# Ten query products of the late half-steps summed whole by VectorE, and the last value product summed in one strided instruction

## The chip, the cores and the metric

The kernel runs on one core of one Trainium2 chip. The core has five engines, each with its own queue of instructions: TensorE (matrix products; PE in the profile, and PEld for its weight loads), VectorE (DVE), ScalarE (ACT), GpSimd (POOL) and SyncE (SP, which here issues most of the DMA transfers). They run side by side and wait for each other through semaphores. The metric is the device time of one execution in microseconds (us); lower is better.

## The reference

Four layers, each added to its input, work on one sequence of 2048 positions with 640 features in float32. Layers 1 and 3 are a local attention, layers 2 and 4 a Fourier mixing; both attention layers use the same weights.

```python
x = A_x
x = x + _A_ref(_layernorm(x, axis=-1), A_wqkv, A_wo)
x = x + _B_ref(_layernorm(x, axis=-1), ...)
x = x + _A_ref(_layernorm(x, axis=-1), A_wqkv, A_wo)
x = x + _B_ref(_layernorm(x, axis=-1), ...)

def _A_ref(x, wqkv, wo):            # H = 32 heads of Dh = 20, W = 8, dil = 2
    ...
    idx = pos[:, None] - off[None, :]            # the 8 positions pos - 0, 2, .. 14
    kg = k[:, :, idx_c, :].reshape(B, H, S, W, Dh)
    vg = v[:, :, idx_c, :].reshape(B, H, S, W, Dh)
    logits = jnp.einsum("bhsd,bhswd->bhsw", q, kg) * scale
    logits = jnp.where(mask[None, None, :, :], logits, -1e9)
    attn = _softmax(logits, axis=-1)
    o = jnp.einsum("bhsw,bhswd->bhsd", attn, vg)
    return (lambda x, *d: x.transpose(*d))(o, 0, 2, 1, 3).reshape(B, S, D) @ wo

def _B_ref(x, dft_seq_re, dft_seq_im, dft_hid_re, dft_hid_im):
    a = jnp.einsum("bsd,ed->bse", x, dft_hid_re)
    b = jnp.einsum("bsd,ed->bse", x, dft_hid_im)
    return jnp.einsum("ts,bse->bte", dft_seq_re, a) - jnp.einsum("ts,bse->bte", dft_seq_im, b)
```

## The kernel before

**Tiling.** The even positions are put ahead of the odd ones, so that a step of two becomes a step of one. A chunk `c` (four of them) is 512 positions: 128 partitions of four neighbouring positions `j`. Every large matrix product is made of three TensorE passes over a high and a low part of each operand; ScalarE makes the high part, and VectorE, GpSimd or TensorE the low one.

**The attention layer** (`layer_a`, lines 242 to 863) is cut into 32 units `u`, each one group of four heads (80 features) of one chunk, and a unit into two half-steps, s = 2u + jp, of two of the four positions. So a layer has 64 half-steps, and what is called a step in the code is one half-step. In the last eight units (`PAIRED`) a unit holds two head groups for the same two positions; the work of a half-step is the same. For each half-step there are:

- a query product (`qk_mul`, L431): VectorE multiplies the queries, which ScalarE has copied into PSUM (`q_copy`, L404), with the window of eight keys, 1280 elements on each partition: 2 positions, 8 window places, 4 heads, 20 features;
- a halving (L433): GpSimd adds the features 10 to 19 of every head to the features 0 to 9, in place;
- a reduction (`qk_red`, L439), one step later: VectorE sums the ten that are left to one logit, 64 logits on each partition;
- the softmax on VectorE and ScalarE (`soft`, L454 to L464, `soft_exp`, L447), once for a unit;
- three steps later a weight product (`av_mul`, L469): VectorE multiplies the attention weights with the window of eight values, 1280 elements again;
- a tree (`av_tree`, L484 to L486): GpSimd adds the eight window places in three sums of 640, 320 and 160 elements; the last one writes 80 features into the output tile `zo`. For the very last product of a layer VectorE makes the three sums itself.

The products lie in four buffers `pr0` to `pr3`, taken in turn; a half-step takes two of them (one for L431, one for L469), so that a buffer comes back after two half-steps. The windows `win` have five buffers, which DMA fills ahead (L417).

**Beside these steps** TensorE makes the query, key and value projections of later chunks (L362), the transposes of inputs and outputs (L327, with L335 for the low part), the output projection (L509, added to the residual by VectorE at L159), and in the late steps it begins the next layer's transform along the sequence (L956). For that one, matrices are loaded (`c_load`, L912) and split by ScalarE (L916) and GpSimd or VectorE (`c_lo`, L943); layer normalised inputs are split by ScalarE (L885) and GpSimd or VectorE (`ln_lo`, L889).

**Order.** In an attention layer the order on all engines is the program's own: a table `plan` gives each piece of work a step and a phase, and `PHASES` orders the phases of a step. Each engine works its list strictly in that order. In a step of odd number the reduction (`red1`) comes after the query product, in one of even number (`red0`) ahead of it. After step 66 the last two output tiles are written out by hand: transposes of `zo` (`pc_pe(67)`), the rest of the output projection and the normalisation.

**Names that the change touches:** `qk_mul`, `qk_red`, `av_tree`, and a new table `WHOLE` beside `LEAD2`. `ly` is 0 in the first attention layer and 1 in the second; `NG` is 32, so `(NG - 1, 1)` is the last half-step.

Of the kernel before, what the change touches and what calls it, by code (L numbers as in the profile page):

```python
# [14 lines left out]
ALU = mybir.AluOpType  # L15
AX = mybir.AxisListType
# [18 lines left out]
FE = 80  # L35
# [8 lines left out]


LEAD2 = (-7, -6, -5, -4, -2, -1, 0, 0, 1, 1, 2, 3, 3, 4, 5, 5)
ZTHIRDS = (
    {49: 3, 50: 3, 51: 2, 53: 3, 54: 1, 56: 3, 57: 6, 58: 3, 59: 4, 60: 2, 61: 1, 62: 3, 63: 4, 64: 1, 55: 0, 52: 0},
    {50: 3, 51: 5, 52: 1, 53: 1, 54: 1, 55: 1, 56: 5, 57: 4, 58: 3, 59: 3, 60: 1, 61: 1, 62: 4, 63: 2, 64: 4},
# [25 lines left out]
def tile_layers(ctx: ExitStack, tc: tile.TileContext, x, wqkv, wo, cs, wre, wim, out):  # L75
    nc = tc.nc
# [13 lines left out]
    def T(shape, tag, dt=F32, bufs=1, pool=None):  # L90
        return (pool or sb).tile(shape, dt, tag=tag, name=nm(tag), bufs=bufs)
# [146 lines left out]
    NG = NC * NE  # L238
# [3 lines left out]
    def layer_a(li, stats, handoff, prev):  # L242
        xin, xout = xs[li], xs[li + 1]
        first = li == 0
        ly = li // 2
# [10 lines left out]
        prq = {}  # L256
        avq = {}
        oo = {}
# [8 lines left out]
        def prod():  # L267
            pcnt[0] += 1
            return T([P, 2, W, FE], f"pr{pcnt[0] % 4}")
# [114 lines left out]
        def half(u, i):  # L384
            if u in PAIRED:
                q, jp = PAIRED[u]
                return 2 * q + i, jp
            return u % NE, i
# [35 lines left out]
        def wview(u, i, t, tail):  # L424
            w, off = win.pop((u, i, t))
            return bass.AP(tensor=w.tensor, offset=w.offset + off, ap=[w.ap[0], [FE, 2], [FE, W]] + tail)

        def qk_mul(u, jp):
            pr = prod()
            q = qs[u][:, 2 * jp : 2 * jp + 2].unsqueeze(2).to_broadcast([P, 2, W, FE])  # L430
            nc.vector.tensor_tensor(pr, q, wview(u, jp, 0, [[1, FE]]), op=ALU.mult)  # L431
            pv = pr.rearrange("p j w (h d) -> p (j w h) d", d=DH)
            nc.gpsimd.tensor_tensor(pv[:, :, 0:10], pv[:, :, 0:10], pv[:, :, 10:20], op=ALU.add)  # L433
            prq[(u, jp)] = pv

        def qk_red(u, jp):
            if jp == 0:
                lgs[u] = T([P, NJ, W, HE], "lg", bufs=2)
            nc.vector.tensor_reduce(  # L439
                lgs[u][:, 2 * jp : 2 * jp + 2].rearrange("p j w h -> p (j w h)"),  # L440
                prq.pop((u, jp))[:, :, 0:10],
                axis=AX.X,
                op=ALU.add,
            )
# [32 lines left out]
        def av_tree(u, i):  # L477
            c = u // NE
            e, jp = half(u, i)
            if e == 0:  # L480
                oo[(c, jp)] = T([P, 2, D], f"zo{(2 * c + jp) % 4}")
            pr = avq.pop((u, i))
            g = nc.vector if (u, i) == (NG - 1, 1) else nc.gpsimd
            g.tensor_tensor(pr[:, :, 0:4], pr[:, :, 0:4], pr[:, :, 4:8], op=ALU.add)  # L484
            g.tensor_tensor(pr[:, :, 0:2], pr[:, :, 0:2], pr[:, :, 2:4], op=ALU.add)  # L485
            g.tensor_tensor(oo[(c, jp)][:, :, e * FE : (e + 1) * FE], pr[:, :, 0], pr[:, :, 1], op=ALU.add)  # L486

        def r_load(c, j, tag="xr"):
            xr[(c, j)] = load_x(xin[c], j, tag)
# [182 lines left out]
        o = NJ * FE + NJ * W * HE  # L672
# [21 lines left out]
        ]  # L694
        gs = list(LEAD0 if first else LEAD2)
        tx = {(0, j): -8 for j in range(NJ)}
        st = 4
        while len(gs) < NGRP:
            if st % 2 == 0 and len(tx) < NC * NJ:
                c, j = divmod(len(tx), NJ)  # L700
# [16 lines left out]
        for u in range(NG):  # L717
            if u in PAIRED:
                for i in range(2):
                    at(2 * u + i - 2, "dmaw", w_load, u, 0, i)  # L720
                    at(2 * u + i + 1, "dmaw", w_load, u, 1, i)
            else:
                at(2 * u - 2, "dmaw", w_load, u, 0)
                at(2 * u + 1, "dmaw", w_load, u, 1)
            at(2 * u - 1, "qc", q_copy, u)
            at(2 * u - 2, "dma", q_load, u)
            for jp in range(2):
                s = 2 * u + jp
                at(s, "qk", qk_mul, u, jp)
                at(s + 1, "red0" if jp else "red1", qk_red, u, jp)  # L730
                at(s + 3, "av0" if jp else "av1", av_mul, u, jp)
                at(s + 3, "av0" if jp else "av1", av_tree, u, jp)
            for i, ph in enumerate(("sA", "sB", "sC")):
                at(2 * u + 2, ph, soft, u, i)
                at(2 * u + 3, ("sD", "sE", "sF")[i], soft, u, 3 + i)
            at(2 * u + 2, "exp", soft_exp, u)
# [65 lines left out]
        last = 66  # L802
        thirds = [t for t, n in ZTHIRDS[ly].items() for _ in range(n)]
        for z, (tag, t) in PRE.items() if first else ():
# [552 lines left out]
```

## Time and profile before

| | us |
|---|---|
| runs before | 1794.40, 1787.53, 1791.88; median 1791.88 |
| the profiled execution, as a run | 1791.85 |
| its span in the profile | 1790.0 |
| mean granted TensorE clock | 0.995 of full speed |

| engine | busy us | share of the span | instructions |
|---|---|---|---|
| TensorE, matmuls (PE) | 1740.7 | 97% | 8798 |
| TensorE, weight loads (PEld) | 1506.0 | 84% | 8798 |
| VectorE (DVE) | 1380.2 | 77% | 2137 |
| ScalarE (ACT) | 813.0 | 45% | 1690 |
| GpSimd (POOL) | 636.4 | 36% | 595 |

A name such as `DVE lg L439` in the profile is an engine, the tile that it writes and the line of the kernel. `lg<-pr 128x64 f32<-128x640 f32 x128 | 103.9, 812 | 18.2` is a group of instructions: output and input by name, their shapes (partitions x elements), how many, busy time in us, the mean of one in ns, and the engine's idle time just before them. Busy times over the span are averages over stages that differ, so the stretches of the attention layers are read by themselves: the first one runs from about 30 to 390 us, the second from about 930 to 1280 us. An instruction's end in the profile can overlap the next one's start by a little, since the engines pipeline.

### The profile page before, as it was taken

Reading aid. Unit: us, or ns where it says so; the run is one execution under the profiler, and the core shown is the slowest. Engines: PE = TensorE matmul, PEld = TensorE weight load, DVE = VectorE, ACT = ScalarE, POOL = GpSimd, SP = SyncE. Lnnn points to the kernel's source line nnn. Section 1 sums busy time; section 2 is a strip of 40 time slices with the busy share of each in tenths; the row PEclk is TensorE's granted clock in tenths of the full one; section 3 lists DMA queues with packets and bytes.
Section 4 is the critical chain, followed back from the end, with each engine's and each line's share of the span. In section 5 each row is a group of like instructions: output and inputs, shape, how many; then the busy total and the mean of one; then the engine's idle time right before and its main releaser. Section 6 shows DMA issues by size and latency. Waiting matters only on the chain.

```text
span 1790.0 us, 26461 instructions
## 1 busy us (share of the span) xinstructions
PE 1740.7 (97%) x8798; PEld 1506.0 (84%) x8798; DVE 1380.2 (77%) x2137; ACT 813.0 (45%) x1690; POOL 636.4 (36%) x595
## 2 busy tenths in 40 slices
PE   9999998989999999999999999999999999999999
PEld 7889887778888888888888889888788888888888
DVE  6999998887767767767728999989777677677683
ACT  4664544454445445445523344444534443443441
POOL 4899999940000000000007998889300000000000
PEclk9999999999999999999999999999999999999999
DMA  7896678757778777787737866687687777876761
GB/s 246 286 313 203 211 212 270 251 183 281 273 251 258 246 265 253 238 272 255 216 107 220 285 205 209 211 303 254 218 298 263 254 226 225 265 230 224 257 208 52
DMA packets 271849, 425.15 MB, mean 238 GB/s; under 512 B 22592, under 2 KB 150592, under 8 KB 271456
## 3 DMA queue, kind: packets, MB, share of 16 engines
q1 hardware_dynamic: 268512, 421.49, 71.9%
q10 hardware_dynamic: 3200, 1.97, 0.4%
q8 instruction: 70, 1.15, 0.3%
q14 instruction: 67, 0.55, 0.1%
HBM read 338.23 MB, written 85.14 MB: 237 GB/s over the span
## 4 chain that ended last, share of the span: by engine, by line
PE 59%; DVE 15%; POOL 10%; DMA 9%; issue 3%; ACT 2%; SPq 0%; ACTq 0%; DVEq 0%; POOLq 0%
PE aux L1034 13%; PE m L362 11%; PE m L1123 10%; PE t L1123 10%; PE pq L1123 5%; PE xt L1123 5%; DVE pr L431 4%; POOL pr L484 3%; DVE pr L469 3%; POOL pr L433 2%; DMA win<-cs_in 2%; POOL pr L485 2%; PE aux L509 2%; DMA xc<-stg 1%; DVE lg L439 1%
## 5 line engine op out<-in xcount | busy, mean ns | idle before, releaser
L362 PE MATMUL m<-r,s 128*128 128x480 f32 x1920 | 438.0, 383 | 4.2 <-ACT s L232 3.7
L362 PEld LDWEIGHTS m<-r,s 128*128 128x128 f32 x1920 | 356.4, 189 | 58.3 <-ACT s L232 4.6
L174 POOL TENSOR_TENSOR stats<-stats,mhalf 128x1 f32<-128x1 f32 (+1 forms) x40 | 29.8, 745 | 564.1 <-ACT stats L170 554.8
L1116 ACT CAST r<-win 128x512 fp32r<-128x512 f32 x248 | 151.2, 619 | 169.2 <-DVE win L1152 78.3
L1034 PE MATMUL aux<-r2a,zo 128*128 128x320 f32 x768 | 226.4, 310 | 0.0
L484 POOL TENSOR_TENSOR pr<-pr 128x640 f32<-128x640 f32 x126 | 205.1, 1628 | 30.6 <-DVE pr L469 29.8
L1034 PE MATMUL aux<-pr,zo 128*128 128x320 f32 x704 | 208.2, 308 | 0.0
L1117 DVE TENSOR_TENSOR r<-win,r 128x512 fp32r<-128x512 f32 x248 | 167.6, 688 | 44.9 <-ACT r L1116 42.9
L431 DVE TENSOR_TENSOR pr<-pq,win 128x1280 f32<-128x1280 f32 x128 | 189.8, 1483 | 15.9 <-ACT pq L404 12.7
L469 DVE TENSOR_TENSOR pr<-pq,win 128x1280 f32<-128x1280 f32 x128 | 190.9, 1491 | 4.3
L433 POOL TENSOR_TENSOR pr<-pr 128x640 f32<-128x640 f32 x128 | 183.8, 1436 | 14.1 <-DVE pr L431 13.7
L1123 PE MATMUL m<-r,r 128*128 128x512 f32 x606 | 156.2, 392 | 0.7 <-DVE r L1117 0.7
L1034 PEld LDWEIGHTS aux<-r2a,zo 128*128 128x128 f32 x768 | 144.1, 188 | 2.0
L1123 PEld LDWEIGHTS m<-r,r 128*128 128x128 f32 x606 | 113.6, 188 | 26.2 <-DVE r L1117 1.0
L1034 PEld LDWEIGHTS aux<-pr,zo 128*128 128x128 f32 x704 | 132.1, 188 | 2.1
L1123 PE MATMUL t<-r,r 128*128 128x512 f32 x483 | 130.7, 393 | 2.3 <-issue 1.3
L956 PE MATMUL m<-s,r 128*128 128x512 f32 x384 | 119.0, 397 | 11.3 <-DMA s<-c0b 3.9
L956 PE MATMUL t<-s,r 128*128 128x512 f32 x384 | 119.2, 398 | 2.3 <-DVE ot L1016 1.5
L439 DVE TENSOR_REDUCE lg<-pr 128x64 f32<-128x640 f32 x128 | 103.9, 812 | 18.2 <-POOL pr L433 18.0
L485 POOL TENSOR_TENSOR pr<-pr 128x320 f32<-128x320 f32 x126 | 112.9, 896 | 9.9
L1123 PEld LDWEIGHTS t<-r,r 128*128 128x128 f32 x483 | 90.5, 188 | 23.7 <-issue 1.7
L369 ACT COPY stg<-m 128x480 f32<-128x480 f32 x128 | 70.9, 554 | 81.6 <-PE m L362 58.9
(285 smaller groups left out, 3227.7 us busy)
## 6 DMA issues: line engine op xcount, KB each, us to landing
win<-cs_in SPq DMA_DIRECT2D x354, 256.0 KB, 4.2
r<-xc SPq DMA_DIRECT2D x240, 256.0 KB, 4.3
win<-kvb SPq DMA_DIRECT2D x96, 440.0 KB, 4.5
xa<-cs_in SPq DMA_DIRECT2D x122, 256.0 KB, 4.3
win<-kvb SPq DMA_DIRECT2D x64, 360.0 KB, 5.1
xc<-stg SPq DMA_DIRECT2D x40, 512.0 KB, 3.8
kvb<-stg SPq DMA_DIRECT2D x60, 320.0 KB, 4.6
xr<-xs SPq DMA_DIRECT2D x41, 320.0 KB, 3.7
```

Source lines behind the costliest of these rows:

```text
L362: nc.tensor.matmul(mt[g][:, : 3 * F], st[:, a, k], wq[q][:, b, k], start=n == 0, stop=n == 14)
L431: nc.vector.tensor_tensor(pr, q, wview(u, jp, 0, [[1, FE]]), op=ALU.mult)
L433: nc.gpsimd.tensor_tensor(pv[:, :, 0:10], pv[:, :, 0:10], pv[:, :, 10:20], op=ALU.add)
L439: nc.vector.tensor_reduce(lgs[u][:, 2 * jp : 2 * jp + 2].rearrange("p j w h -> p (j w h)"), prq.pop((u, jp))[:, :, 0:10], axis=AX.X, op=AL ...
L469: nc.vector.tensor_tensor(pr.rearrange("p j w (h d) -> p j w h d", d=DH), lgs[u][:, 2 * jp : 2 * jp + 2].unsqueeze(4).to_broadcast([P, 2, ...
L484: g.tensor_tensor(pr[:, :, 0:4], pr[:, :, 0:4], pr[:, :, 4:8], op=ALU.add)
L485: g.tensor_tensor(pr[:, :, 0:2], pr[:, :, 0:2], pr[:, :, 2:4], op=ALU.add)
L956: self.last = nc.tensor.matmul(self.z[t][k], self.xn[c][:, a, j, k * P : (k + 1) * P], self.ct[s][:, b], start=s == 0 and i == 0, stop=s = ...
L1034: self.last = nc.tensor.matmul(self.ym[e][:, :320], zt[(k, a, ri)][:, j2 * P : (j2 + 1) * P], w[:, e * 320 : (e + 1) * 320], start=(k, a, ...
L1116: nc.scalar.copy(hi, raw)
L1117: nc.vector.tensor_tensor(lo, raw, hi.bitcast(F32), op=ALU.subtract)
L1123: nc.tensor.matmul(bank, w(a, kb), hl[b], start=start and (a, b) == (0, 0), stop=stop and (a, b) == (1, 0),)
```

## The change

For ten half-steps, listed in `WHOLE` (eight in the first attention layer: 43, 45, 47, 49, 51, 55, 57 and 59; two in the second: 51 and 57), GpSimd's halving is left out, and VectorE's reduction reads all twenty features of a head in place of ten. For the last weight product of each attention layer, VectorE's three sums become one reduction over the window axis, whose eight terms lie 80 elements apart. Everything else, and the order of the remaining instructions on every engine, is as it was. The kernel after has 10 GpSimd instructions fewer and 4 VectorE instructions fewer.

```diff
+WHOLE = ((43, 45, 47, 49, 51, 55, 57, 59), (51, 57))
...
             pv = pr.rearrange("p j w (h d) -> p (j w h) d", d=DH)
-            nc.gpsimd.tensor_tensor(pv[:, :, 0:10], pv[:, :, 0:10], pv[:, :, 10:20], op=ALU.add)
+            if 2 * u + jp not in WHOLE[ly]:
+                nc.gpsimd.tensor_tensor(pv[:, :, 0:10], pv[:, :, 0:10], pv[:, :, 10:20], op=ALU.add)
+                pv = pv[:, :, 0:10]
             prq[(u, jp)] = pv
...
                 lgs[u][:, 2 * jp : 2 * jp + 2].rearrange("p j w h -> p (j w h)"),
-                prq.pop((u, jp))[:, :, 0:10],
+                prq.pop((u, jp)),
                 axis=AX.X,
                 op=ALU.add,
...
             pr = avq.pop((u, i))
-            g = nc.vector if (u, i) == (NG - 1, 1) else nc.gpsimd
+            o = oo[(c, jp)][:, :, e * FE : (e + 1) * FE]
+            if (u, i) == (NG - 1, 1):
+                nc.vector.tensor_reduce(o, pr.rearrange("p j w f -> p j f w"), axis=AX.X, op=ALU.add)
+                return
+            g = nc.gpsimd
             g.tensor_tensor(pr[:, :, 0:4], pr[:, :, 0:4], pr[:, :, 4:8], op=ALU.add)
             g.tensor_tensor(pr[:, :, 0:2], pr[:, :, 0:2], pr[:, :, 2:4], op=ALU.add)
-            g.tensor_tensor(oo[(c, jp)][:, :, e * FE : (e + 1) * FE], pr[:, :, 0], pr[:, :, 1], op=ALU.add)
+            g.tensor_tensor(o, pr[:, :, 0], pr[:, :, 1], op=ALU.add)
```

## The prediction

> **What bounds the kernel now.** I read the page first, then busy time by stretch, then the chain of waits and who waited for whom in the late half-steps, and last the single instructions. The 40 slices of the page are 44.75 us each.
>
> ```profile
> PE   9999998989999999999999999999999999999999
> DVE  6999998887767767767728999989777677677683
> POOL 4899999940000000000007998889300000000000
> ```
>
> TensorE is full nearly everywhere. GpSimd works only in the two attention layers (slices 0 to 8 and 21 to 28), and late in them it is as full. The change lies there, so I cut out that part.
>
> ```profile
> 244.00:304.90 60.90, 51.49 (x256) 44.77 (x255) 53.00 (x78) 29.11 (x71) 59.09 (x55) 0.92 0.81 262
> 304.90:346.00 41.10, 40.42 (x218) 35.46 (x217) 32.35 (x52) 20.10 (x49) 40.08 (x37) 1.00 0.78 262
> 1200.00:1236.00 36.00, 35.76 (x193) 31.25 (x191) 32.67 (x50) 19.33 (x46) 34.31 (x30) 1.00 0.82 280
> ```
>
> Columns: length, then busy PE, PEld, DVE, ACT, POOL, then granted clock, DMA share, GB/s. From 244 to 304.9 us GpSimd is busy 59.09 of 60.90 us and TensorE idles 9.4. From 304.9 to 346, and in the second layer from 1200 to 1236, TensorE idles under 0.7 us: there a faster GpSimd shortens nothing at once. The chain of waits from 244 to 333 us agrees; its longest pieces are nearly all GpSimd's (start, us, what), as these.
>
> ```profile
> 272.61 1.54 POOL pr L484
> 275.70 1.53 POOL r L889
> ```
>
> What this costs VectorE (who waited for whom: total us, times, longest); the first row is from 244 to 304.9 us, the next two from 304.9 to 346, the last two from 1183 to 1260.
>
> ```profile
> DVE lg L439 <- POOL pr L433: 5.9, 5, 1.7
> DVE lg L439 <- POOL pr L433: 4.1, 2, 2.5
> DVE r L159 <- PE aux L509: 4.0, 4, 1.7
> DVE lg L439 <- POOL pr L433: 2.7, 2, 1.8
> DVE pr L431 <- DMA win<-kvb: 2.3, 1, 2.3
> ```
>
> The reduction of the logits waits for the halving 5.9 + 4.1 = 10.0 us in layer one and 2.7 in layer two. Counting the reductions in program order, these nine waits belong to half-steps 43, 45, 47, 49, 51, 57, 59 and to 51, 57: exactly those that the change touches, but for half-step 55, which has no wait.
>
> **The change part by part: the ten products.** Removed: ten halvings on GpSimd. Longer: ten reductions on VectorE, from 640 to 1280 elements. By line and shape in the late half-steps (busy us, mean ns, idle before):
>
> ```profile
> L433 POOL TENSOR_TENSOR pr<-pr 128x640 f32<-128x640 f32 x18 | 25.6, 1421 | 0.0
> L439 DVE TENSOR_REDUCE lg<-pr 128x64 f32<-128x640 f32 x18 | 14.7, 814 | 10.0 <-POOL pr L433 10.0
> L431 DVE TENSOR_TENSOR pr<-pq,win 128x1280 f32<-128x1280 f32 x18 | 26.7, 1484 | 0.5 <-ACT pq L404 0.5
> ```
>
> GpSimd gives up 8 x 1.42 = 11.4 us in layer one and 2.8 in layer two. The longer reduction isn't in the trace. Another VectorE instruction over 1280 elements takes 1.48 us; twice L439 is 1.63, the upper bound. Its 20 terms lie side by side, as the ten did, so I take 1.48: 0.67 more than 0.81. Each half-step then gains VectorE its wait and costs it 0.67 us. Layer one: 10.0 - 8 x 0.67 = 4.6 us (3.4 with 1.63; at most 10.0, if every extra fell into VectorE's 4.0 us of waits for TensorE and other slack). Layer two: half-step 51 gains 0.9 - 0.67 = 0.2, but the 2.3 us wait for a window load follows and takes it; half-step 57 gains 1.8 - 0.67 = 1.1.
>
> No instruction changes its place on any engine, and no DMA is added or moved past another. One wait is new in form: after a whole reduction VectorE has no word from GpSimd, so the next weight product (L469) waits for itself on GpSimd's tree that read the same buffer two half-steps before. Behind it on VectorE stand the rest of the softmax and the output adds, for which ScalarE and TensorE wait. The rows show half-step 57: that older tree ended at 329.3, and the weight product comes only after 333.5, behind the longest of the waits.
>
> ```profile
> 328.76 0.54 POOL L486 TENSOR_TENSOR zo<-pr 128x160 f32<-128x160 f32 x1
> 331.31 1.42 POOL L433 TENSOR_TENSOR pr<-pr 128x640 f32<-128x640 f32 x1
> 332.77 0.82 DVE L439 TENSOR_REDUCE lg<-pr 128x64 f32<-128x640 f32 x1 [2.49 <-POOL pr L433]
> 333.50 1.48 DVE L431 TENSOR_TENSOR pr<-pq,win 128x1280 f32<-128x1280 f32 x1
> ```
>
> I cost that wait at nothing: over 4 us cover it here, and 2.49 fewer would leave about 2. If GpSimd's backlog used that up, the wait returned, to the 10.0 us at most.
>
> Can TensorE use the gain? Of the 4.6 us, 5.9 - 5 x 0.67 = 2.5 arise before 304.9 us, where TensorE idles 9.4. The other 2.1 arise where TensorE is full; VectorE runs ahead there, and TensorE takes it up afterwards, where it waits for VectorE, or for ScalarE, which waits for VectorE. The first three rows are from 304.9 to 358 us, the last from 1200 to 1246.
>
> ```profile
> PE aux L509 <- DVE xa L159: 2.1, 1, 2.1
> PE aux L335 <- ACT s L331: 0.7, 1, 0.7
> PE aux L509 <- ACT ot L350: 0.7, 1, 0.7
> ```
>
> ```profile
> PE aux L509 <- DVE xa L159: 1.3, 1, 1.3
> ```
>
> That is 3.5 us for the 2.1 of layer one and 1.3 for the 1.1 of layer two. I keep 4.6 and 1.1.
>
> **The last value product.** Three VectorE sums at the end of each layer become one reduction over 1280 elements, its eight terms 320 bytes apart. TensorE's last transposes wait for it and for GpSimd's last tree.
>
> ```profile
> 377.40 1.17 DVE L484 TENSOR_TENSOR pr<-pr 128x640 f32<-128x640 f32 x1
> 377.97 1.34 POOL L485 TENSOR_TENSOR pr<-pr 128x320 f32<-128x320 f32 x1
> 379.69 0.53 DVE L486 TENSOR_TENSOR zo<-pr 128x160 f32<-128x160 f32 x1
> 380.10 0.73 PE L327 MATMUL pq<-ident,zo 128*128 128x128 f32 x4 [0.89 <-POOL zo L486]
> ```
>
> ```profile
> 1266.62 1.49 DVE L484 TENSOR_TENSOR pr<-pr 128x640 f32<-128x640 f32 x1
> 1268.89 0.33 DVE L486 TENSOR_TENSOR zo<-pr 128x160 f32<-128x160 f32 x1
> 1269.27 0.55 PE L327 MATMUL pq<-ident,zo 128*128 128x128 f32 x3 [0.38 <-DVE zo L486]
> ```
>
> ```profile
> L460 DVE TENSOR_REDUCE pq<-lg 128x16 f32<-128x128 f32 x9 | 3.6, 395 | 0.9
> L485 POOL TENSOR_TENSOR pr<-pr 128x320 f32<-128x320 f32 x17 | 14.9, 875 | 1.3
> ```
>
> The three sums end 2.8 and 2.6 us after they begin. The strided reduction takes 1.48 us by L431's row. The only strided reduction shown, L460, takes 0.395 for 128 elements: L439 and 1.48 give (1.48 - 0.81) / 640 = 1.05 ns an element and 0.14 us fixed; if the rest of L460 goes by the element, that is 2.0 ns, and 1280 of them take 2.7 us. L460 is the same operation with a step between its terms, so I take 2.7: VectorE itself gains nothing. GpSimd does: its second sum took 1.34 us beside VectorE's sums against 0.875 elsewhere, about 0.5 us less in layer one, where TensorE waits 0.89 for GpSimd. I take 0.4 us for both layers (from 0.1 lost, 2.7 against 2.6, to 1.3 won, TensorE's two waits).
>
> [...]
>
> **The sum.** 4.6 + 1.1 + 0.4 = 6.1 us. The profiled execution took 1791.85 us (a span of 1790.0 and 1.85 around it); the median of the runs is 1791.88. 1791.85 - 6.1 = 1785.75, say 1785.8 us. With the bounds (ten times 0.15 us more for the reductions; 0.9 less from the tail, 1.3 less if the extras of half-steps 55 and 57 vanish in waits for TensorE) and some 2 us for the runs' spread, the forecast's own range is 1782 to 1789.
>
> **The rivals.** First: the clock pauses go too, which is faster still. From 244 to 304.9 us the granted clock is 0.92: TensorE lost 0.08 x 60.9 = 4.9 us, in three stretches of half clock. One of them, with the stretch before it:
>
> ```profile
> 280.99:284.40 3.41, 1.41 (x6) 1.19 (x7) 1.74 (x4) 0.00 (x0) 3.33 (x5) 1.00 0.44 138
> 284.40:287.82 3.42, 3.42 (x10) 2.62 (x9) 2.83 (x4) 2.30 (x7) 3.26 (x4) 0.50 0.85 282
> ```
>
> TensorE idles 2.0 of 3.41 us, and the next 3.42 run at half clock. The idle times behind two of the three hang on GpSimd and on ScalarE behind VectorE, from 240 to 382 us:
>
> ```profile
> PE m L956 <- POOL s L943: 3.7, 2, 2.1
> PE t L335 <- ACT s L331: 2.4, 1, 2.4
> ```
>
> Both shrink. If all three stretches go and TensorE sets the end: 1785.8 - 4.9 = 1780.9. Against it: GpSimd bounds there, so part of that loss is slack. [...]
>
> Second: the gain is hidden. TensorE is full from 304.9 to 346 us and in layer two; if VectorE's lead is lost there, 2.5 + 0.4 = 2.9 us remain: 1789.0.
>
> Third, slower: VectorE sets the pace. It is busy 53.00 of 60.90 us; if its wait for GpSimd comes back as waits for TensorE or window loads, nothing is won, and ten reductions cost 6.7 us more on it: 1798.6, and 1.7 more if a new gap halves the clock. It decides once under 6.7 of the 12.7 us of wait are really lost. Against it: beside this wait VectorE has only 4.5 us of others from 244 to 346 us.
>
> Fourth, the change only renames the wait: L469 waits for GpSimd where L439 did, 1791.9.
>
> **How the numbers follow.** The forecast 0.46, the clock 0.24, hidden 0.17, slower 0.08, renamed 0.05. The range, 1778 to 1794, holds the clock case with 3 us of spread below and no change with 2 above. About 0.5%, 9.0 us, is what a measurement of this kernel can tell from no change. Faster than 1782.9: nine tenths of the clock case (0.22) and a fifth of the forecast (0.09), 0.31. Slower than 1800.8 takes the third rival with a lost clock and part of the spread: 0.05. The rest is 0.64.
>
> **What would show it.** Right: late in the layers L439 comes in two lengths, 0.81 and 1.48 us, with no wait for GpSimd before the long ones; TensorE idles less than 7 us from 244 to 300; layer one ends 4 to 6 us earlier. Wrong: long reductions of over 1.7 us; VectorE waiting several us more for TensorE, or at L469 for GpSimd; or a tail reduction of over 3 us, which goes straight onto TensorE's last wait.

## The result, and the profile after

The kernel after took 1785.46 us (median of 12 runs, 1780.83 to 1790.76), the kernel before 1790.84 in 12 runs beside it (1786.92 to 1794.7). The ratio is 0.9972, with a 95% interval of 0.9961 to 0.9982: by it 5.0 us less, between 3.2 and 7.0 (the medians lie 5.4 apart). The profiled execution took 1783.08 us, with a span of 1781.3 and a granted clock of 0.995 as before. The forecast was 1785.8.

The page of after, the same three lines of slices (here 44.5 us each):

```profile
PE   9999998999999999999999999999899999999999
DVE  6999999987867767767738999989777677677683
POOL 4899999840000000000017999989200000000000
```

GpSimd's digit falls from 9 to 8 in slice 7 (the first is 0) and VectorE's rise from 8 to 9 in slices 6 and 7: work has moved from the one to the other. The same stretches as before, cut 2.3 us earlier in the first layer and 8.4 earlier in the second (columns as above):

```profile
244.00:302.60 58.60, 50.83 (x255) 43.67 (x255) 55.70 (x79) 29.49 (x71) 53.32 (x51) 0.92 0.84 267
302.60:343.70 41.10, 40.45 (x217) 35.49 (x215) 36.04 (x54) 19.70 (x48) 36.61 (x35) 1.00 0.79 270
1191.60:1227.60 36.00, 35.69 (x190) 30.97 (x189) 34.43 (x51) 19.22 (x46) 34.16 (x31) 1.00 0.85 288
```

The first stretch is 2.3 us shorter with the same matmuls but one on TensorE. TensorE still idles 7.8 of its 58.6 us (9.4 of 60.9 before), and its granted clock is 0.92 again. The second is as long as before: TensorE is full, GpSimd has 3.5 us less to do (36.61 against 40.08) and VectorE 3.7 more (36.04 against 32.35). Who waits for whom on VectorE, after; the first two rows are from 244 to 302.6 us, the next two from 302.6 to 343.7, the last two from 1174 to 1250:

```profile
DVE r L160 <- PE aux L516: 0.7, 1, 0.7
DVE pr L432 <- ACT pq L405: 0.5, 1, 0.5
...
DVE r L160 <- PE aux L516: 4.3, 3, 2.0
DVE pr L432 <- ACT pq L405: 0.4, 1, 0.4
...
DVE r L160 <- PE aux L516: 2.4, 3, 1.7
DVE pr L432 <- DMA win<-kvb: 2.2, 1, 2.2
```

The 10.0 us of waits for GpSimd's halving are gone from these stretches, and no other wait for GpSimd stands in their place. The reductions by line and shape, over the whole of after:

```profile
L442 DVE TENSOR_REDUCE lg<-pr 128x64 f32<-128x640 f32 x118 | 95.8, 812 | 4.5 <-POOL pr L435 4.3
L442 DVE TENSOR_REDUCE lg<-pr 128x64 f32<-128x1280 f32 x10 | 14.8, 1477 | 0.0
L488 DVE TENSOR_REDUCE zo<-pr 128x160 f32<-128x1280 f32 x2 | 4.7, 2369 | 0.0
```

The whole reduction takes 1.48 us, the strided one 2.37. Last the ends of the two layers, instruction by instruction (start, length, engine, line; a bracket is the idle time just before and what ended it):

```profile
375.45 2.37 DVE L488 TENSOR_REDUCE zo<-pr 128x160 f32<-128x1280 f32 x1
376.02 0.88 POOL L492 TENSOR_TENSOR pr<-pr 128x320 f32<-128x320 f32 x1
376.98 0.53 POOL L493 TENSOR_TENSOR zo<-pr 128x160 f32<-128x160 f32 x1
377.56 0.86 PE L328 MATMUL pq<-ident,zo 128*128 128x128 f32 x4 [0.31 <-POOL zo L493]
...
1256.93 2.37 DVE L488 TENSOR_REDUCE zo<-pr 128x160 f32<-128x1280 f32 x1
1259.36 0.55 PE L328 MATMUL pq<-ident,zo 128*128 128x128 f32 x3 [0.36 <-DVE zo L488]
```

GpSimd's second sum takes 0.88 us beside the strided reduction, where it took 1.34 beside VectorE's sums, and TensorE's wait for GpSimd falls from 0.89 to 0.31.

Where the time went, from the starts of single instructions. TensorE's last transposes of layer one start at 377.56 instead of 380.10, 2.5 us earlier; 0.3 of that was there before the first changed half-step. In layer two the way from the query product of half-step 50 to the transposes at the end is 92.34 us (1167.02 to 1259.36) instead of 94.44 (1174.83 to 1269.27), 2.1 us less. The layers thus give 2.3 + 2.1 = 4.4 of the 8.7 us by which the two profiled spans differ (1790.0 and 1781.3). Not all of the 2.1 is the change's: 1.3 lie from half-step 56 to 63 and 0.2 behind 63, but 0.5 from 50 to 56, and that stretch takes 34.0 to 38.6 us in the fourteen traces of this text, and 34.3 to 36.3 in the four of kernels whose layer two is unchanged up to there. The rest of the 8.7 us lies outside the changed stretches, where the change touches nothing, and comes and goes: the kernel before had a stretch of 3.4 us at half clock at 895 us, which after lacks, and which is worth 1.7, half of its length. The experiments therefore look at the layers' own stretches beside the times.

### The profile page after: what moved, and what is told of

It reads as the page before. It is cut to its first block, busy times and chain, and to the rows that moved or that the text cites. A ratio compares the mean times of both kernels' runs of the same rounds, so it can differ in the third digit from the quotient of the medians.

```text
span 1781.3 us, 26451 instructions
## 1 busy us (share of the span) xinstructions
PE 1740.1 (98%) x8798; PEld 1505.6 (85%) x8798; DVE 1386.1 (78%) x2133; ACT 813.7 (46%) x1690; POOL 622.1 (35%) x585
## 4 chain that ended last, share of the span: by engine, by line
PE 60%; DVE 18%; DMA 10%; POOL 5%; issue 4%; ACT 2%; SPq 1%; DVEq 0%; ACTq 0%; POOLq 0%
PE aux L1041 13%; PE m L363 11%; PE m L1130 10%; PE t L1130 10%; PE pq L1130 5%; PE xt L1130 5%; DVE pr L432 4%; PE aux L516 3%; DVE pr L472 3%; DMA xc<-stg 3%; DMA win<-cs_in 2%; DVE lg L442 2%; POOL pr L491 2%; POOL pr L435 1%; POOL pr L492 1%
## 5 line engine op out<-in xcount | busy, mean ns | idle before, releaser
L491 POOL TENSOR_TENSOR pr<-pr 128x640 f32<-128x640 f32 x126 | 207.0, 1643 | 40.3 <-DVE pr L472 39.8
L435 POOL TENSOR_TENSOR pr<-pr 128x640 f32<-128x640 f32 x118 | 168.2, 1426 | 12.9 <-DVE pr L432 12.4
L442 DVE TENSOR_REDUCE lg<-pr 128x64 f32<-128x640 f32 (+1 forms) x128 | 110.5, 864 | 4.5 <-POOL pr L435 4.3
```

Of the source, the lines that this page charges most:

```text
L442: nc.vector.tensor_reduce(lgs[u][:, 2 * jp : 2 * jp + 2].rearrange("p j w h -> p (j w h)"), prq.pop((u, jp)), axis=AX.X, op=ALU.add,)
```

## The experiments

All times are medians of 12 runs, each beside 35 runs of the kernel before on the same chip. A difference of means (12 runs less 35) carries a standard error of 0.7 to 0.9 us.

| kernel | us | before, us | ratio, 95% interval | means, us |
|---|---|---|---|---|
| only 43 to 51 of layer one | 1789.23 | 1792.81 | 0.9995, 0.9982 to 1.0007 | -2.1 |
| only 55, 57, 59 of layer one | 1793.20 | 1792.81 | 1.0009, 0.9997 to 1.0020 | +0.9 |
| only 51, 57 of layer two | 1789.41 | 1792.81 | 0.9991, 0.9981 to 1.0001 | -2.6 |
| only the two strided reductions | 1791.91 | 1792.81 | 1.0003, 0.9990 to 1.0016 | +0.4 |
| the kernel after once more | 1788.44 | 1791.80 | 0.9987, 0.9974 to 0.9999 | -2.6 |
| after without 55, 57, 59 | 1787.32 | 1791.80 | 0.9975, 0.9964 to 0.9986 | -4.4 |
| after, GpSimd loaded again | 1792.07 | 1791.80 | 1.0000, 0.9987 to 1.0012 | +0.7 |
| without 55, 57, 59, `c_lo` ahead | 1788.87 | 1791.80 | 0.9981, 0.9968 to 0.9994 | -3.1 |
| without 55, 57, 59, TensorE lightened | 1790.26 | 1791.92 | 0.9989, 0.9976 to 1.0002 | -2.0 |
| with them, TensorE lightened | 1789.52 | 1791.92 | 0.9981, 0.9968 to 0.9994 | -3.2 |
| without them, TensorE kept busy | 1788.36 | 1791.92 | 0.9987, 0.9974 to 1.0000 | -3.4 |
| after, last product laid out anew | 1787.27 | 1791.92 | 0.9973, 0.9957 to 0.9988 | -4.6 |

From the profiled executions, one of each kernel, the length of three stretches, from the start of one query product to that of another (us):

| kernel | layer one, 40 to 52 | layer one, 54 to 63 | layer two, 56 to 63 |
|---|---|---|---|
| before | 64.26 | 55.01 | 40.35 |
| only 43 to 51 | 61.76 | 55.52 | 40.58 |
| only 55, 57, 59 | 64.28 | 55.84 | 40.34 |
| only layer two | 64.24 | 55.37 | 39.15 |
| only the strided reductions | 64.26 | 54.55 | 40.59 |
| after | 61.52 | 55.32 | 39.02 |
| after once more | 61.46 | 55.59 | 39.07 |
| after without 55, 57, 59 | 63.45 | 54.41 | 39.07 |
| GpSimd loaded again | 63.03 | 55.22 | 41.07 |
| `c_lo` ahead | 61.51 | 54.24 | 39.04 |
| lightened, without 55, 57, 59 | 61.67 | 55.59 | 39.37 |
| lightened, with them | 61.02 | 54.38 | 39.18 |
| kept busy | 63.21 | 54.37 | 38.95 |
| last product laid out anew | 63.12 | 55.83 | 38.94 |

### The four parts alone

The first four kernels each hold one part of the change. Their edits are to the table `WHOLE`, with the three sums on VectorE kept in the first three; the fourth has an empty table and the strided reduction:

```diff
-WHOLE = ((43, 45, 47, 49, 51, 55, 57, 59), (51, 57))
+WHOLE = ((43, 45, 47, 49, 51), ())
```

> Only half-steps 43, 45, 47, 49 and 51 of layer one are summed whole; all else, the last product too, is as before. Theory A (the forecast: each changed half-step is worth its wait for GpSimd less 0.67 us, wherever it lies): 5.9 - 5 x 0.67 = 2.5 us less in layer one, nothing in layer two, the whole run 2.5 us faster. Theory B (only what is won before TensorE is full, ahead of 305 us, counts): the same 2.5 us, and VectorE stays 2 to 2.7 us ahead up to the end of layer one. Theory C (the gain is the clock's: fewer pauses, no matter which half-steps): no lead of VectorE that can be traced to the half-steps, and a total that goes by the number of half-clock stretches, 1.7 us each.

```diff
+WHOLE = ((55, 57, 59), ())
```

> Only half-steps 55, 57 and 59 of layer one are summed whole; all else is as before. Theory A: 4.1 - 3 x 0.67 = 2.1 us faster. Theory B: TensorE is full from 305 to 346 us, so VectorE's lead after half-step 57 (about 1.2 us) is given back as a wait for TensorE by half-step 60; layer one ends 0 to 0.7 us earlier, the run is the same within 1 us. Theory C: as the clock falls, 0 to 3.4 us either way.

```diff
+WHOLE = ((), (51, 57))
```

> Only half-steps 51 and 57 of layer two are summed whole; all else is as before. Theory A: 1.1 us faster (0.2 of half-step 51 is taken by the window load behind it). Theory B: 0.5 us or less, since TensorE is full around half-step 57 there as well. What the two profiles of before and after suggest: VectorE gains 0.3 to 0.5 at half-step 51 and 1.2 to 1.3 at 57, keeps both to the end of the layer, 1.7 us in all, of which the loads behind the layer take some back.

```diff
+WHOLE = ((), ())
```

> Only the last weight product of each layer is changed (one strided reduction for three sums); the halvings are all kept. All theories: the reduction takes 2.37 us as in the profile after (1.48 would be its length without a price for the stride), GpSimd's last tree gets back its 0.875 and 0.53 us in layer one, TensorE's wait before its last transposes there falls from 0.89 to 0.3 us: 0.4 to 0.6 us in layer one, 0 to 0.2 in layer two, the run 0.4 to 0.8 us faster, which is at the edge of what five rounds can show.

By the ratios no part alone differs from before beyond its interval; the means add up to -3.4 us, against -5.5 and -2.6 us in the two measurements of the whole. (The mean of layer two alone, -2.6 with an error of 0.7, is twice what its stretch shows below.) The stretches say more. Half-steps 43 to 51 shorten 40 to 52 by 2.5 us (64.26 to 61.76), and in after by 2.7; the three kernels without them stay within 0.02 us of before. The next two half-steps, 52 to 54, scatter: 11.9 to 13.0 us (13.9 with GpSimd loaded again), and 12.8 with the strided reductions alone, whose code is before's up to there. Half-step 57 of layer two shortens 56 to 63 by 1.2 us, and against before by 1.0 to 1.4 in every kernel that has it but the one with GpSimd loaded again. Half-steps 55, 57 and 59 shorten nothing: 54 to 63 takes 55.84 us with them alone, 55.01 without. The strided reduction shortens the way from the start of the last sum to the output projection behind the transposes in layer one from 3.89 us (377.40 to 381.29) to 3.44 (377.81 to 381.25), too little for the runs to see.

Why do 55, 57 and 59 bring nothing, when the waits they remove were 4.1 us? By stretch, from half-step 54 to 63, first before, then the kernel with these three alone (columns as above):

```profile
308.42:363.43 55.01, 51.28 (x277) 44.86 (x277) 46.37 (x71) 23.97 (x59) 53.23 (x48) 1.00 0.76 252
```

```profile
308.98:364.81 55.83, 51.99 (x269) 46.15 (x269) 50.21 (x71) 24.63 (x61) 50.04 (x46) 0.94 0.74 248
```

TensorE's clock differs between the two, 1.00 and 0.94, but isn't the reason: where it is 0.97 in this stretch, the five kernels without these three take 54.2 to 55.5 us (only 43 to 51, only the strided reductions, after without the three, `c_lo` ahead, kept busy), and the three with them 55.3 to 55.8 (after twice, and laid out anew).

VectorE works 3.8 us more (46.37 to 50.21) in as many instructions, and three longer reductions are only 2.0 of it. The other 1.8 lies in three instructions that become slower beside GpSimd's. Single instructions of both engines show it; before:

```profile
335.79 1.56 POOL L889 TENSOR_TENSOR r<-r,r 128x640 fp32r<-128x640 f32 x1
337.05 0.99 DVE L889 TENSOR_TENSOR r<-r,r 128x640 fp32r<-128x640 f32 x1
337.30 1.14 POOL L174 TENSOR_TENSOR stats<-stats,mhalf 128x1 f32<-128x1 f32 x1
338.41 1.42 POOL L433 TENSOR_TENSOR pr<-pr 128x640 f32<-128x640 f32 x1
...
348.63 0.98 DVE L889 TENSOR_TENSOR r<-r,r 128x640 fp32r<-128x640 f32 x1
348.88 2.00 POOL L433 TENSOR_TENSOR pr<-pr 128x640 f32<-128x640 f32 x1
```

and after:

```profile
333.47 1.41 POOL L435 TENSOR_TENSOR pr<-pr 128x640 f32<-128x640 f32 x1
333.71 1.86 DVE L896 TENSOR_TENSOR r<-r,r 128x640 fp32r<-128x640 f32 x1
334.83 2.17 POOL L491 TENSOR_TENSOR pr<-pr 128x640 f32<-128x640 f32 x1
...
344.91 1.40 POOL L435 TENSOR_TENSOR pr<-pr 128x640 f32<-128x640 f32 x1
345.12 1.88 DVE L896 TENSOR_TENSOR r<-r,r 128x640 fp32r<-128x640 f32 x1
346.27 2.15 POOL L491 TENSOR_TENSOR pr<-pr 128x640 f32<-128x640 f32 x1
346.92 2.05 DVE L950 TENSOR_TENSOR s<-stg,s 128x512 fp32r<-128x512 f32 x1
```

The low part of the layer norm (`ln_lo`, L889 and L896) takes VectorE 0.99 and 0.98 us before. The first falls at the end of a GpSimd instruction and beside a small one on a single column; the second starts 0.25 us ahead of GpSimd's halving, and it is the halving that then takes 2.00 us instead of 1.42. After, with GpSimd's backlog gone, both start 0.2 us behind a halving. Now the halvings take their 1.4 us and VectorE 1.86 and 1.88, and L950 takes 2.05 instead of 1.90: 1.9 us more on VectorE. The kernel with 55, 57 and 59 alone shows the same (1.89 us on average, and 2.06); every kernel without these three has 0.96 to 1.00. So VectorE gets 4.1 us of waits back and pays 2.0 + 1.9. The run with GpSimd loaded again, further down, bears out that the lost backlog makes the difference: it has these three whole too, but GpSimd is behind as before, and the two instructions take 1.20 and 0.82 us (VectorE is busy 48.56 us from 54 to 63, 2.2 more than before, of which the longer reductions are 2.0). In these rows the time goes with the order in which `ln_lo` and a halving start: where VectorE is 0.25 us ahead it takes 0.98 us and GpSimd 2.00, where it is 0.2 us behind it takes 1.86 and 1.88 and GpSimd 1.41 and 1.40.

### Is it GpSimd's time or VectorE's waiting for a result

The kernel after once more gives the second measurement of the whole; beside it stand after without 55, 57 and 59, and after with GpSimd's time put back. The last makes the first sum of the tree twice in ten steps, so that GpSimd has as much to do as before (1.57 us for each halving of 1.42), while VectorE still waits for no halving of these ten:

```diff
             g.tensor_tensor(pr[:, :, 0:4], pr[:, :, 0:4], pr[:, :, 4:8], op=ALU.add)
+            if 2 * u + i + 3 in WHOLE[ly]:
+                g.tensor_tensor(pr[:, :, 0:4], pr[:, :, 0:4], pr[:, :, 4:8], op=ALU.add)
```

> The changed kernel once more, beside the same runs of the kernel before, so that the parts measured one by one and the whole stand on one footing. The parts gave, against the mean of all runs of before taken beside them, about -2 (half-steps 43 to 51), +1 (55, 57, 59), -2.5 (layer two) and 0 us (the last product), -3.5 in sum with some 1.5 us of uncertainty. Theory A and B: 3 to 5 us faster again, VectorE 2 to 3 us ahead at half-step 54 of layer one, and between half-steps 57 and 61 a lead that comes and goes. Theory C (clock alone): the leads differ from those of the first profile.

> As the changed kernel, but half-steps 55, 57 and 59 of layer one keep GpSimd's halving. Theory A (every half-step is worth its wait less 0.67 us): 2.1 us slower than the changed kernel. Theory B (what is won while TensorE is full is given back): the same as the changed kernel within 1 us, or up to 1 us faster, since 55 only adds 0.67 us to VectorE; VectorE's lead at half-step 62 is 2.5 to 3 us in both.

> As the changed kernel, but GpSimd gets the time back that it was spared: in each of the ten steps it makes the first sum of the tree twice (1.57 us each; the window places 4 to 7 count twice there), while VectorE still sums the ten products whole and waits for no halving. Theory P (GpSimd's chain sets the pace of the late half-steps, 59.09 of 60.90 us busy): the gain of layer one is gone or turned round: VectorE's lead at half-step 54 is below 1 us, its waits for GpSimd come up at the other reductions, and the run is at best 1 us faster than before. Theory V (what counts is that VectorE doesn't wait for the halving behind GpSimd's backlog): VectorE keeps 2 us or more of lead at half-step 54 and the run is 3 to 5 us faster than before, like the changed kernel.

With GpSimd loaded again the whole gain is gone (ratio 1.0000): of the 1.2 us won up to half-step 52 nothing is left at 54, since 52 to 54 takes 13.9 us instead of 11.9. VectorE's waits for GpSimd, from 244 to 346 us and from 1174 to 1250:

```profile
DVE lg L442 <- POOL pr L435: 9.7, 6, 2.9
...
DVE lg L442 <- POOL pr L435: 1.3, 1, 1.3
```

9.7 of the 10.0 us in layer one are back, now at the reductions of half-steps that kept their halving (46, 50, 52, 53, 56, 58). What the change wins is GpSimd's time, not the shorter chain from product to reduction: as long as GpSimd is behind, VectorE waits for it at the next halved product.

After without 55, 57 and 59 is no slower than after (0.9975, against 0.9972 and 0.9987). In its profile 40 to 52 is only 0.8 us shorter than before, and the kernels kept busy and laid out anew have about as little, 1.1. These three share a wait of over 2 us that is at most 0.7 in the others. The last one has the same code as after up to the end of the layer, so the pair shows it (ScalarE's split of a loaded matrix, and the query product of half-step 50); first after:

```profile
282.42 0.62 ACT L923 CAST s<-stg 128x512 fp32r<-128x512 f32 x1 [4.52 <-DMA stg<-cs_in]
283.40 1.49 DVE L432 TENSOR_TENSOR pr<-pq,win 128x1280 f32<-128x1280 f32 x1 [0.50 <-ACT pq L405]
```

and the kernel with the last product laid out anew:

```profile
284.64 0.62 ACT L926 CAST s<-stg 128x512 fp32r<-128x512 f32 x1 [6.12 <-DMA stg<-cs_in]
285.62 1.49 DVE L432 TENSOR_TENSOR pr<-pq,win 128x1280 f32<-128x1280 f32 x1 [2.09 <-ACT pq L405]
```

The load of a matrix lands 2.2 us later in this execution. Behind its split on ScalarE stands the copy of the queries, and behind that VectorE, which loses 1.6 of its lead of 2.7 us. In before the same split started at 284.70 us and cost VectorE 0.52, since VectorE came late itself. So this load is what is late next: the first five half-steps give 2.5 to 3.2 us where it lands early and about 1 where it lands late. What sets its landing wasn't found.

### A shorter wait of TensorE for the split matrices

In the early stretch TensorE waits for GpSimd's split of the matrices (`c_lo`). Here that split is put ahead of the tree in GpSimd's list:

```diff
-WHOLE = ((43, 45, 47, 49, 51, 55, 57, 59), (51, 57))
+WHOLE = ((43, 45, 47, 49, 51), (51, 57))
...
-                at(t - 1, "misc", handoff.c_lo, z, z < NJ or z in (11, 12))
+                early = z < NJ or z in (11, 12)
+                at(t - 1, "sA" if early else "misc", handoff.c_lo, z, early)
```

> As early_two, and in layer one GpSimd makes the low part of the next layer's first matrices (six instructions of 1.26 us) ahead of the tree of the step in place of behind it. In before and after alike TensorE waits 3.7 us for two of them around 283 and 292 us, and the clock falls to half behind these waits. If TensorE's idle time is what is left to win there (theory B): those two waits fall below 1 us, one half-clock stretch fewer, 2 to 4 us faster than early_two in layer one, if GpSimd's trees, 1.3 us later, hold nobody up. If GpSimd's chain sets the pace (theory P): the same or slower, since GpSimd does the same work.

TensorE's waits from 238 to 304 us in this kernel:

```profile
PE aux L516 <- ACT s L351: 2.4, 1, 2.4
PE m L964 <- POOL s L951: 1.9, 1, 1.9
PE t L336 <- ACT s L332: 1.8, 1, 1.8
PE aux L328 <- POOL zo L493: 1.1, 1, 1.1
```

One of the two waits for the split went (3.7 us in two before, 1.9 in one here), and a new one of 1.1 us for the tree's output came. Layer one has two slices at half clock up to 305 us, one fewer than without the edit, but the kernel after once more has two as well without it. The time is no better than without the edit (0.9981, against 0.9975).

### Does a full TensorE hide the late half-steps

To test the other half of the reason, TensorE was relieved: the third of the three passes of the transform is left out for seven of its blocks in layer one. The pair differs in 55, 57 and 59 alone.

```diff
+            if self.li == 1 and t == 0 and p == 2 and 3 <= s <= 9:
+                return
```

> As early_two (half-steps 43 to 51 of layer one and 51, 57 of layer two whole, the new last product), with TensorE relieved where it is full: the third pass of seven of the next layer's products (z 3 to 9, 35 matmuls of some 0.22 us) is left out in layer one, which falls between 300 and 350 us. It is the reference for light_late. Theories A and B: TensorE is no longer full between 305 and 346 us, and the run is some 5 to 8 us faster than early_two, if nothing else is full there; VectorE then waits at half-steps 57 and 59 for GpSimd's halving, 1.5 us or more each.

> As light_early with half-steps 55, 57 and 59 whole too, so that the two differ by these alone. Theory B (a full TensorE took the gain of these three back): with TensorE relieved they are now worth what theory A gave, 1 to 2.1 us faster than light_early, and VectorE keeps its lead from half-step 57 to 63. If they are worth nothing here either, TensorE isn't what took it, and VectorE itself or ScalarE is.

By stretch from half-step 54 to 63, first without the three, then with them:

```profile
305.85:361.44 55.59, 47.23 (x234) 41.51 (x234) 46.30 (x71) 24.53 (x61) 53.72 (x49) 0.88 0.75 249
```

```profile
305.13:359.52 54.39, 45.52 (x234) 39.89 (x234) 50.13 (x73) 24.40 (x61) 48.31 (x44) 0.91 0.76 254
```

Here the three shorten the stretch by 1.2 us (55.59 to 54.39), though VectorE pays the same 3.8 us more as above. With TensorE full they did not (55.01 to 55.84). The means of the runs point the same way, 1.2 us, within their error. But the pair differs in its clock as well (0.88 and 0.91): the kernel without the three has four slices of 3.41 us at half clock in this stretch and the one with them three, and one slice costs 1.7 us, more than the 1.2. So it isn't shown that a full TensorE hides the gain. That the lightened kernels would themselves be 5 to 8 us faster was missed: TensorE then waits 4.0 us for a load of matrices, and runs more of the stretch at half clock (0.88, where before had 1.00), so that it wasn't really relieved. The row is from 304 to 358 us of the lightened kernel without the three:

```profile
PE m L965 <- DMA s<-c0b: 4.0, 1, 4.0
```

### The clock pauses

Four idle matrix products before each of three waits were to keep TensorE's clock up:

```diff
+            if t == 0 and (self.li, s, p) in ((1, 0, 0), (1, 2, 1), (3, 2, 0)):
+                jb = self.z[t][0] if s == 0 else pt([P, 512], "aux0")
+                cj = s - (self.li == 3)
+                for _ in range(4):
+                    nc.tensor.matmul(jb, self.xn[0][:, 0, cj, 0:P], self.ct[cj][:, 0], ...)
```

> As early_two, with four more matmuls (some 1.1 us), whose results are overwritten or unused, ahead of three of TensorE's waits: at its first and third product of the next layer in layer one (waits of 0.6 to 3.1 us around 281 and 292 us) and at the third in layer two (2.5 to 3 us around 1184 us). Theory C' (TensorE's idle time brings the half clock): the stretch of half clock behind 1184 us goes, and one of those between 281 and 303 us; TensorE loses 1.7 us less for each, and the run is 1.5 to 3.5 us faster than early_two. If the half clock doesn't hang on idle time, or has slack around it: the same as early_two within 1 us, or slower by the added matmuls.

Not settled. The products did not fill the waits: TensorE still waited 2.2, 1.9 and 1.9 us from 238 to 304 us, layer one had three slices at half clock by 305 us as before, layer two still one at 1185 us (two without the edit), and the time can't be told from that without the edit (0.9987, against 0.9975).

### The stride of the last sum

After, with the last weight product written so that the eight window places lie side by side, and read so by the reduction:

```diff
+            if (u, jp) == (NG - 1, 1):
+                o = bass.AP(tensor=pr.tensor, offset=pr.offset, ap=[pr.ap[0], [W * FE, 2], [1, W], [W * DH, HE], [W, DH]])
...
-                nc.vector.tensor_reduce(o, pr.rearrange("p j w f -> p j f w"), axis=AX.X, op=ALU.add)
+                nc.vector.tensor_reduce(o, pr.rearrange("p j w f -> p j (w f)").rearrange("p j (f w) -> p j f w", w=W), axis=AX.X, op=ALU.add)
```

> As the changed kernel, but the last weight product of each layer is written with its eight window places side by side, so that the reduction reads 1280 elements in order and the product writes with a step of 32 bytes. If the step of the reads is what makes the reduction 2.37 us long: 1.48 us here, and the product's write either stays at 1.49 us or takes over some of the price. TensorE's last wait for VectorE in layer two (0.36 us) goes, the run is 0 to 0.5 us faster than the changed kernel, too little to be told by the runs. If the reduction's length has another reason (eight terms to a sum): it stays near 2.4 us.

The end of layer one in this kernel:

```profile
375.99 2.67 DVE L475 TENSOR_TENSOR pr<-pq,win 128x1280 f32<-128x1280 f32 x1
378.70 1.49 DVE L491 TENSOR_REDUCE zo<-pr 128x160 f32<-128x1280 f32 x1
380.24 0.55 PE L328 MATMUL pq<-ident,zo 128*128 128x128 f32 x3 [0.30 <-DVE zo L491]
```

The reduction falls from 2.37 to 1.49 us, so the stride costs it 0.88; but the product that now writes with the stride takes 2.67 instead of 1.48. The price has moved from the read to the write, 0.3 us dearer, and the time (0.9973) can't be told from after's.

## Why the prediction was right in its sum and wrong in a part

**Right: the whole reduction.** 1.48 us was taken and 1.48 measured. No wait for GpSimd is left before one.

**Right in size, with a condition that it lacked: the first five of layer one.** 2.5 us were to arise before 304.9 us; 40 to 52 is 2.7 us shorter in after and 2.5 with these five alone. Of after's 2.7, 0.7 is gone by half-step 54, in a wait for TensorE (12.67 us from 52 to 54, 11.93 before; 12.81 with the strided reductions alone, so that this may be scatter), and where a matrix load lands late only 0.8 to 1.1 us arise at all. The prediction asked which wait for a window load follows, and not which other load stands ahead of VectorE on ScalarE.

**Wrong: 55, 57 and 59.** The step was "Each half-step then gains VectorE its wait and costs it 0.67 us", and after it "VectorE runs ahead there, and TensorE takes it up afterwards". Of the 2.1 us nothing came from 54 to 63. The first sentence fails because the cost is 0.67 and, for these three together, 1.9 us more in VectorE instructions that now run beside GpSimd's: 4.1 - 2.0 - 1.9 = 0.2. The prediction had a row of such a kind (GpSimd's second sum, 1.34 us beside VectorE's sums against 0.875 elsewhere), and used it for the tail alone. The second sentence fails too. TensorE's wait for VectorE's output add, which was to be filled up, grew from 2.1 to 2.8 us in after. Whether a full TensorE would have taken the gain without these 1.9 us isn't shown: the pair with a lightened TensorE differs in clock, and of the runs with the three, only the one with GpSimd loaded again is without them (1.20 and 0.82 us for `ln_lo`), and there the waits are back.

**Slightly low: layer two.** Predicted 1.1 us from half-step 57; 56 to 63 is 1.2 us shorter with the two half-steps alone and 1.3 in after. Whether the 0.2 us of half-step 51 went into the wait for a window load isn't shown: that wait is 2.2 us now and was 2.3, and the stretch around it scatters by far more.

**Right in size, by other numbers: the tail.** 0.4 us was taken. The strided reduction takes 2.37 us, between the 1.48 and 2.7 that bounded it, so VectorE gains 0.4 us of its 2.8 in layer one. GpSimd's second sum gets back 0.46 of the 0.5 predicted (that a reduction beside it would leave it at its 0.875 us was the author's estimate; in after it takes 0.88), and the output projection of layer one comes 0.4 us sooner after the start of the last sum, with the tail alone and in after. In layer two the transposes come 0.2 us sooner (2.65 to 2.43). By times the tail alone is 1.0003: not to be told from nothing.

**The marks.** TensorE was to idle under 7 us from 244 to 300; it idles 7.8 there, and 8.4 before. Layer one was to end 4 to 6 us earlier; it ends 2.5 earlier. Both missed, the second by about the 2.1 us of the three late half-steps; the first lies ahead of them, in waits of TensorE that hardly changed (3.7 us for GpSimd's split before and after).

**The sum.** 6.1 us were predicted. The layers of the profile give 4.4, of which the 0.5 from 50 to 56 of layer two isn't shown to be the change's; the two measurements 5.0 and 2.3 us by their ratios (1790.84 x 0.0028 and 1791.8 x 0.0013). That the first median came within 0.4 us of the forecast is partly luck: it holds some time from outside the changed stretches, which isn't the change's. Why the stretches there differ by several us from profile to profile stays open, apart from the pause at 895 us.

**The rivals.** That the clock pauses go: fell. Layer one has 10.2 us at half clock up to 305 us before and 10.2 after, at other places (6.8 in after once more), and both measurements of after have one slice more at 354 or 355 us. That the gain is hidden: right in size for the three late half-steps of layer one, where by the sum above the 1.9 us in VectorE instructions beside GpSimd's account for it, and wrong for layer two, so that the time lies between it and the forecast. That VectorE sets the pace: fell; its price was real, but only where there was little to win. That the wait is renamed: fell, and the run with GpSimd loaded again shows what it would have taken, one more GpSimd sum of 1.57 us in each of the ten steps; the wait then comes back at the next halved products, and not at the weight product.

No kernel here beats after beyond the error. After without 55, 57 and 59 does as well with three changed half-steps fewer.

## What to carry to other kernels

Work moved from a late engine to a waiting one paid here where the engine after them had idle time in that same stretch (half-steps 43 to 51: 2.5 to 2.7 us, with TensorE idle for 9.4 of 60.9); where TensorE is full, look for the place at which a lead would be taken up (half-step 57 of layer two won its 1.2 us there, the three late ones of layer one nothing). Count what the instructions around the moved work will then meet: here the lost backlog changed which of two engines starts first, and that cost VectorE 1.9 us, about as much as the longer instructions did (2.0). When medians differ by less than the parts' errors, the lengths of the touched stretches tell the parts apart.

## What the runs showed of the hardware

TensorE fell to half clock after stretches in which it idled for some 2 us only. In after, cut into slices on the 3.41 us grid on which the changes of the clock lie, one slice idles 2.0 us and three at half clock follow:

```profile
289.32:292.74 3.42, 1.39 (x7) 1.07 (x7) 3.35 (x6) 0.54 (x3) 2.45 (x4) 1.00 0.96 293
292.74:296.15 3.41, 3.19 (x13) 2.37 (x11) 3.29 (x4) 2.39 (x9) 3.25 (x4) 0.50 0.95 331
296.15:299.56 3.41, 1.46 (x5) 1.46 (x6) 3.31 (x5) 2.94 (x8) 3.25 (x5) 0.50 0.96 310
299.56:302.98 3.42, 3.42 (x14) 3.42 (x14) 2.66 (x6) 2.59 (x4) 3.34 (x4) 0.50 0.99 378
```

In before, a slice of the same grid with 1.6 us of idle time left the clock at 1.00 in the next:

```profile
352.67:356.08 3.41, 1.77 (x8) 1.11 (x6) 3.24 (x7) 0.00 (x0) 2.96 (x4) 1.00 0.36 108
356.08:359.49 3.41, 2.96 (x20) 2.97 (x21) 3.34 (x8) 0.43 (x1) 3.19 (x4) 1.00 0.54 162
```

The other traces agree. Cut on their own grids, the fourteen traces of this text have 55 slices at full clock with over 1.9 us of idle time, and all are followed by half clock; of the slices with less than 1.79 us one is (1.36 us), and between the two 10 of 18 are. Of the slices at half clock the 12 that idle 0.5 us or more are all followed by another at half clock, and of the 60 others only the second row of after above, with 0.2 us. In these traces it thus matters where a wait falls on the grid: in before, one of 2.09 us from 354.44 us lies across a border of it, 1.64 and 0.45 us on its two sides, and the clock stays at 1.00; one of 2.06 us from 280.93 has 2.00 of them in one slice, and the next, full of work, runs at half clock, which is worth 1.7 us (half of its 3.41). The other numbers not expected were 0.88 us for a stride of 320 bytes in a reduction of 1280 elements (2.37 against 1.49), and 1.2 for a strided write of as many (2.67 against 1.48).
